# Decayed keys of 16 units turned by VectorE in 32 x 32 blocks and carried through DRAM

## The chip, the cores and the metric

The kernel runs on one core of one Trainium2 chip. Its time is the device time of one execution in microseconds (us), the median of several runs. TensorE (PE in the profile) multiplies, VectorE (DVE) and ScalarE (ACT) work on rows of up to 128 partitions, GpSimd (POOL) does a little of the same, and SyncE (SP) issues the DMAs in this kernel. Each engine works through its own instructions in their order and waits on semaphores for the others.

## What is computed

An attention with a state that decays channel by channel, and an MLP with ELU on its result. In the kernel the sequence is cut into chunks of 128 tokens, in which the decays are multiplied up, so that a chunk is a masked product of 128 x 128 scores, a product with the state, and an update of the state.

```python
def _attn_setup():
    batch, n_heads, seq, head_dim = (4, 8, 768, 48)
    ...

def _attn_ref(r, k, v, w, u) -> np.ndarray:
    B, H, S, D = r.shape
    state = np.zeros((B, H, D, D), dtype=np.float32)
    y = np.zeros_like(r)
    for t in range(S):
        kt, vt, rt, wt = (k[:, :, t], v[:, :, t], r[:, :, t], w[:, :, t])
        cur = np.einsum('bhd,bhe->bhde', u[None] * kt, vt)
        y[:, :, t] = np.einsum('bhd,bhde->bhe', rt, state + cur)
        state = wt[:, :, :, None] * state + np.einsum('bhd,bhe->bhde', kt, vt)
    return y.astype(np.float32)

def _moe_setup():
    n_tokens, d_model, d_ff = (3072, 384, 2048)
    ...

def _moe_ref(x, w_in, w_out) -> np.ndarray:
    h = x @ w_in
    alpha = 1.0
    g = np.where(h > 0.0, h, alpha * (np.exp(np.minimum(h, 0.0)) - 1.0))
    return (g @ w_out).astype(np.float32)

def reference(**kwargs):
    ...
    attn_out = _attn_ref(**attn_kwargs)
    B, H, S, D = attn_out.shape
    x = np.ascontiguousarray(attn_out.transpose(0, 2, 1, 3)).reshape(B * S, H * D)
    return _moe_ref(x=x, **moe_kwargs)
```

## The kernel before

A unit is one chunk c (6 of 128 tokens) of one batch b (4): unit i = 4c + b, 24 units. A unit holds 8 heads as 4 pairs p; a pair's two heads of 48 channels stand in 112 partitions (0 to 47 and 64 to 111; the rows between repeat channels of the first head). Keys and receptances come as `kr`, 112 channel rows of 4 x 128 tokens each, the decays as `w`, the values `v` in token rows.

Attention tasks of a unit, by the names that stand in the tables: `es` and `gs` (VectorE, scans that multiply up the decays, lines 435 and 445), `kh` and `rh` (VectorE, keys and receptances times them), `rk`, `rku`, `md`, `sp` (the diagonal with u), `s` (TensorE, scores, line 526), `mk` (VectorE, copy of the scores under the mask, two per unit, line 539), `t` (TensorE, four transposes that turn the decayed keys from channel rows to token rows in PSUM, line 544, for the units of chunks 0 to 4), `kt` (ScalarE, their copy to SBUF, line 549), `v` (TensorE, line 567, scores times values and state times receptances), `u` (TensorE, line 589, the outer products of keys and values, for two units at a time, named by the second), `up` (VectorE, state plus outer products), `pc` and `sc` (decay of the state), `xh` and `xl` (the result as a rounded part and a rest), `fl` (a check of the range).

The MLP runs over 105 steps n: `g1` (TensorE, line 263: 9 matmuls of one 128-wide slice f of the hidden layer), `r1`, `r2` (ScalarE), `stt` (VectorE, line 279), `gh` (ScalarE) and `gl` (VectorE, line 305), `g2` (TensorE, line 319: 9 matmuls into the sums `acc`). A chunk's 4 x 128 tokens are 512 columns; in chunks 0 and 1 the first slices are done in two halves of 256. The first five steps of chunk 0 use plain float32 (lines 269 and 294). The MLP of a chunk follows its attention, so that chunk c's MLP and chunk c + 1's attention share the engines.

The weights come as `raw` f (768 KB each, 16 of them) and are split into two parts: `a` (ScalarE), `cc` (VectorE, line 622), `wh` (ScalarE, line 627), `wl` (VectorE, line 631). These tasks lie in the first hundred microseconds; g1 of slice f needs wl f. raw 14 goes into a buffer that cc 11 frees, raw 15 into one that cc 12 frees.

Nothing is scheduled at run time. `ORDER` holds for each engine a line of task names, and each engine issues its tasks in that order; for SP the line holds the loads (`ld_w`, `ld_kr`, `ld_rk`, `ld_v`, `raw`) and the `store` of results. `Plan.order` merges the lines, and `hold` says which tasks must be done before a buffer is taken again (`SLOTS` counts the buffers: 3 of kr, 2 of kt, 5 PSUM banks `pa`). The last step of all is g2.104, behind which the last sums are copied and stored.

Of the kernel before, what the change touches and what calls it, by code (L numbers as in the profile page):

```python
# [8 lines left out]
F32 = mybir.dt.float32  # L9
# [10 lines left out]
B, H, S, D = 4, 8, 768, 48  # L20
DM, DFF = 384, 2048
P = 128
# [32 lines left out]
def _pieces():  # L55
    res = []
    for h in range(H):
# [15 lines left out]
UP = ["ACT"] * 4  # L73

# [6 lines left out]
SLOTS = dict(w=2, kr=3, rk=2, v=4, eg=2, md=2, am=2, kt=2, pa=5, wg=2, wt=2, m=2, gh=2, gl=2, x=2, acc=1, raw0=1, x0=1, x1=1, x1a=1, x1b=1, wl10=1, wl11=1, wl12=1, wl13=1, wl14=1, wl15=1)  # L81
# [8 lines left out]
    SP=(  # L90
# [261 lines left out]
def rwkv_elu_kernel(ctx, tc, wkr, rk, vp, u, gkrw, gv, gu, wp, out):  # L352
# [301 lines left out]
    for u_ in units:  # L654
# [35 lines left out]
        if c < NC - 1:  # L690
            add(("t", i), "PE", lambda u_=u_: trans(u_), [("kh", i), ("const",)])
            add(("kt", i), "ACT", lambda u_=u_: trans_out(u_), [("t", i)])
# [234 lines left out]
```

## Time and profile before

| | |
|---|---|
| runs of the kernel | 497.98, 498.17, 500.63 us; median 498.17 |
| the profiled execution | 499.62 us, its span 497.7 |
| TensorE clock granted | 0.998 of 2.4 GHz |
| TensorE busy | 489.3 us, 98 % |
| VectorE busy | 325.7 us, 65 % |
| ScalarE busy | 275.3 us, 55 % |
| GpSimd busy | 74.8 us, 15 % |

A busy share is an average over the span. The page's slices and the table by stretches tell how it is spread, and the list of waits tells for whom an engine stood still. Matmuls are pipelined: the records of neighbours overlap, and a pause shorter than the modelled end of a matmul is seen only in the starts. Where the text speaks of a step it means the time from one start to the next.

### The profile page before, as it was taken

The numbers are of one execution on the slowest core, as the hardware profiler recorded it, in microseconds if no ns is written. First come the engines' busy times: TensorE is split into PE (matmuls) and PEld (weight loads), VectorE is DVE, ScalarE is ACT, GpSimd is POOL, SyncE is SP. The second block draws the span as 40 slices with busy tenths as digits, with TensorE's granted clock in tenths as the row PEclk, the third lists the DMA queues.
The fourth block names the chain that finished last, engine by engine and source line by source line (L and its number), as shares of the span: only waits on it lengthen the run. The fifth ranks groups of instructions, "written<-read, shape, count | busy, mean of one in ns | idle before, by whom it ended". The sixth has DMA issues, their size and how long they took to land.

```text
span 497.7 us, 10425 instructions
## 1 busy us (share of the span) xinstructions
PE 489.3 (98%) x4305; PEld 412.3 (83%) x4305; DVE 325.7 (65%) x518; ACT 275.3 (55%) x553; POOL 74.8 (15%) x84
## 2 busy tenths in 40 slices
PE   8899999999999999999999999999999999999996
PEld 8689878789888888888888888888888888888885
DVE  6899999997888667647786478655562552324232
ACT  3999999776653444734453463444633444435434
POOL 3001032043004205113240341003000000000000
PEclk9999999999999999999999999999999999999999
DMA  8977864515223224225430423013112000010002
GB/s 277 299 262 244 291 227 148 159 52 146 62 73 95 65 69 148 78 61 169 118 101 22 126 96 112 0 39 109 43 24 79 1 3 0 20 46 1 0 0 68
DMA packets 18725, 48.96 MB, mean 98 GB/s; under 512 B 2160, under 2 KB 4336, under 8 KB 18672
## 3 DMA queue, kind: packets, MB, share of 16 engines
q1 hardware_dynamic: 18384, 47.84, 30.3%
q8 instruction: 36, 0.59, 0.5%
q10 hardware_dynamic: 288, 0.39, 0.2%
q14 instruction: 17, 0.14, 0.1%
HBM read 43.50 MB, written 4.72 MB: 97 GB/s over the span
## 4 chain that ended last, share of the span: by engine, by line


## 5 line engine op out<-in xcount | busy, mean ns | idle before, releaser
L263 PE MATMUL ph<-xh,w_h 128*128 128x512 f32 (+1 forms) x300 | 114.0, 380 | 0.0
L319 PE MATMUL acc<-gh,w_h 128*128 128x512 f32 (+1 forms) x299 | 113.4, 379 | 0.0
L319 PE MATMUL acc<-gl,w_h 128*128 128x512 f32 (+1 forms) x299 | 112.7, 377 | 0.1
L263 PE MATMUL ph<-xl,w_h 128*128 128x512 f32 (+1 forms) x300 | 112.7, 376 | 0.0
L263 PE MATMUL ph<-xh,w_l 128*128 128x512 f32 (+1 forms) x300 | 112.6, 375 | 0.0
L319 PE MATMUL acc<-gh,w_l 128*128 128x512 f32 (+1 forms) x299 | 112.3, 376 | 0.0
L279 DVE SCALAR_TENSOR_TENSOR m<-m,ph 128x512 f32<-128x512 f32 (+1 forms) x100 | 63.8, 647 | 72.9 <-ACT m L276 72.5
L305 DVE TENSOR_TENSOR gl<-m,gh 128x512 fp32r<-128x512 f32 (+1 forms) x100 | 65.8, 663 | 67.8 <-ACT gh L301 67.0
L301 ACT CAST gh<-m 128x512 fp32r<-128x512 f32 (+1 forms) x100 | 58.6, 590 | 90.9 <-PE acc L319 65.5
L273 ACT ACTIVATE m<-ph 128x512 f32<-128x512 f32 (+1 forms) x100 | 56.5, 568 | 88.6 <-PE ph L263 66.9
L319 PEld LDWEIGHTS acc<-gl,w_h 128*128 128x128 f32 x299 | 56.3, 188 | 10.9 <-DVE gl L305 0.9
L263 PEld LDWEIGHTS ph<-xh,w_h 128*128 128x128 f32 x300 | 56.5, 188 | 10.4 <-issue 0.2
L263 PEld LDWEIGHTS ph<-xh,w_l 128*128 128x128 f32 x300 | 56.5, 188 | 10.3
L319 PEld LDWEIGHTS acc<-gh,w_h 128*128 128x128 f32 x299 | 56.3, 188 | 10.4
L263 PEld LDWEIGHTS ph<-xl,w_h 128*128 128x128 f32 x300 | 56.5, 188 | 9.8
L319 PEld LDWEIGHTS acc<-gh,w_l 128*128 128x128 f32 x299 | 56.3, 188 | 10.1
L276 ACT ACTIVATE m<-m 128x512 f32<-128x512 f32 (+1 forms) x105 | 61.1, 594 | 1.4
L505 POOL TENSOR_SCALAR_AFFINE_SELECT am<-md 128x512 f32<-128x512 f32 x32 | 24.1, 776 | 156.2 <-PE pa_y L567 98.3
L464 POOL TENSOR_TENSOR rk<-rk 128x384 f32<-128x384 f32 x20 | 22.9, 1156 | 162.6 <-DMA rk<-in_rk_dram 115.7
L435 DVE TENSOR_TENSOR_SCAN eg<-w,reset 112x516 f32<-112x516 f32 x24 | 30.7, 1277 | 3.2 <-DMA w<-in_wkr_dram 1.8
L445 DVE TENSOR_TENSOR_SCAN eg<-w,reset 112x516 f32<-112x516 f32 x24 | 31.0, 1294 | 0.8
L539 DVE COPY_PREDICATED am<-upper,pa_s 128x512 f32<-128x512 uint32 x40 | 28.0, 730 | 5.2 <-PE pa_s L526 5.2
(86 smaller groups left out, 498.6 us busy)
## 6 DMA issues: line engine op xcount, KB each, us to landing
kr<-in_wkr_dram SPq DMA_DIRECT2D x23, 448.0 KB, 5.5
rk<-in_rk_dram SPq DMA_DIRECT2D x20, 384.0 KB, 3.4
wrawx<-in_wp_dram SPq DMA_DIRECT2D x10, 767.8 KB, 6.6
v<-in_vp_dram SPq DMA_DIRECT2D x24, 256.0 KB, 4.3
w<-in_wkr_dram SPq DMA_DIRECT2D x24, 226.2 KB, 3.8
wraw<-in_wp_dram SPq DMA_DIRECT2D x6, 767.8 KB, 4.5
out_dram<-o SPq DMA_DIRECT2D x9, 256.0 KB, 3.8
out_dram<-o SPq DMA_DIRECT2D x15, 128.0 KB, 2.2
```

Source lines behind the costliest of these rows:

```text
L263: nc.tensor.matmul(ph, w[f][:, 0, k], x_[:, k, :], start=(k == n == 0), stop=(k == NK - 1 and n == 2))
L273: act(s["m"], s["ph"], AF.Relu, scale=-1.0)
L276: act(s["m"], s["m"], AF.Exp, scale=-1.0)
L279: stt_(s["m"], s["m"], -1.0, s["ph"], ALU.add, ALU.max)
L301: nc.scalar.copy(s["gh"], s["m"])
L305: nc.vector.tensor_tensor(s["gl"], s["m"], s["gh"].bitcast(F32), ALU.subtract)
L319: nc.tensor.matmul(a_, w[f][:, 1, m], g[:, s_], start=(begin and n == 0), stop=(stop and n == 2))
L435: nc.vector.tensor_tensor_scan(out=flat(eg[:, 0]), data0=u_["w"][:, 1:W1][:, ::-1], data1=flat(reset[:, 0]), initial=0.0, op0=ALU.mult, op ...
L445: nc.vector.tensor_tensor_scan(out=flat(u_["eg"][:, 1]), data0=u_["w"][:, 0:W1 - 1], data1=flat(reset[:, 1]), initial=0.0, op0=ALU.mult, o ...
L464: eng.tensor_tensor(u_["rk"][:, 0], u_["rk"][:, 0], u_["rk"][:, 1], ALU.mult)
L505: nc.gpsimd.affine_select(out=am, in_=u_["md"][:, q::2].unsqueeze(2).broadcast_to([P, NP, C]), pattern=[[0, NP], [1, C]], compare_op=ALU.i ...
L539: nc.vector.copy_predicated(am.rearrange("t (z p) n -> t z p n", z=2), uppers, windows(pa))
```

## The change

For units 4 to 19 (`VIA`) the tasks `t` (TensorE) and `kt` (ScalarE) are replaced by three:

- `tr` (VectorE): one transpose instruction over 128 partitions and 512 columns, which turns each 32 x 32 block by itself. Its source is the decayed keys, read so that every fourth token makes a block; its target `kq` holds, for each block of 32 channels, token rows in 32 partitions. There is one buffer kq.
- `kd` (SP): a DMA that writes kq (256 KB) to a DRAM buffer.
- `kt` (SP): four DMAs, one for each block of 32 channels, that read it back with the 128 tokens in 128 partitions, in runs of 32 elements (128 bytes) in SBUF.

`kt` in SBUF is now 64 wide per head instead of 48. `kr` is loaded with 128 rows (16 rows repeated at the end) in these units, since the transpose works on whole blocks of 32. `u` waits for the new kt as it did for the old one. All lines of `ORDER` are new: besides the new names, the old ones stand in another order on every engine. The steps of the MLP are the same.

```diff
--- before.py
+++ after.py
@@ -71,6 +71,7 @@
 FILL = {('t', 0): 1, ('pd', 1): 5, ('s', 1): 3, ('g1', 0): 1}
 DIAG = ["PE"] * 4 + ["POOL"] * 20
 UP = ["ACT"] * 4
+VIA = [0] * 4 + [1] * 16 + [0] * 4
 
 
 F32A = 5
@@ -78,96 +79,97 @@
-SLOTS = dict(w=2, kr=3, rk=2, v=4, eg=2, md=2, am=2, kt=2, pa=5, wg=2, wt=2, m=2, gh=2, gl=2, x=2, acc=1, raw0=1, x0=1, x1=1, x1a=1, x1b=1, wl10=1, wl11=1, wl12=1, wl13=1, wl14=1, wl15=1)
+SLOTS = dict(w=2, kr=3, rk=2, v=4, eg=2, md=2, am=2, kt=2, kq=1, kd=4, pa=5, wg=2, wt=2, m=2, gh=2, gl=2, x=2, acc=1, raw0=1, x0=1, x1=1, x1a=1, x1b=1, wl10=1, wl11=1, wl12=1, wl13=1, wl14=1, wl15=1)
...
-        "raw.11 ld_kr.5 raw.12 ld_kr.7 ld_rk.6 raw.14 raw.13 ld_w.6 raw.15 ld_rk.7 ld_kr.6 ld_w.8 ld_v.7 ld_kr.10 ld_v.6 "
...
+        "raw.13 ld_w.6 ld_v.5 ld_kr.5 raw.12 ld_rk.6 kd.4 raw.14 kt.4 kd.5 raw.15 kt.5 ld_v.7 ld_v.6 ld_kr.6 ld_w.7 "
...
@@ -365,6 +367,7 @@
     ml = pool("ml", 3)
     ps_acc = pool("ps_acc", 1, space=PS)
     ps_h = ps_a = pool("ps_a", SLOTS["pa"], space=PS)
+    drm = pool("drm", 1, space=bass.MemoryType.DRAM)
     tt, stt, act = nc.vector.tensor_tensor, nc.vector.scalar_tensor_tensor, nc.scalar.activation
     flags = kp.tile([R2, NU], F32, name="flags")
     good = kp.tile([1, 1], I32, name="good")
@@ -415,16 +418,19 @@
         c, b = u_["c"], u_["b"]
         if n in WKR:
             lo, hi = WKR[n]
-            t, src = ld.tile([R2, hi - lo], F32, tag=n, name=n, bufs=SLOTS[n]), wkr[c, b, :, lo:hi]
+            rows = P if n == "kr" else R2
+            t, src = ld.tile([rows, hi - lo], F32, tag=n, name=n, bufs=SLOTS[n]), wkr[c, b, 0:rows, lo:hi]
         elif n == "rk":
             t, src = ld.tile([P, 2, DM], F32, tag=n, name=n, bufs=SLOTS[n]), rk[c, b]
         else:
             t, src = ld.tile([P, 4 * P], F32, tag=n, name=n, bufs=SLOTS[n]), vp[c, b]
         if n == "kr":
             m = K1 + R1 if u_["i"] else K1 + R1 + 2 * NP
-            nc.sync.dma_start(t[:, 0:m], src[:, 0:m])
-            u_["k"], u_["r"] = (t[:, x:x + K1].rearrange("d (p t) -> d p t", p=NP) for x in (0, K1))
-            u_["ru"] = t[:, K1 + R1:]
+            rows = P if VIA[u_["i"]] else R2
+            nc.sync.dma_start(t[0:rows, 0:m], src[0:rows, 0:m])
+            u_["kx"] = t[:, 0:K1]
+            u_["k"], u_["r"] = (t[0:R2, x:x + K1].rearrange("d (p t) -> d p t", p=NP) for x in (0, K1))
+            u_["ru"] = t[0:R2, K1 + R1:]
         else:
             nc.sync.dma_start(t, src)
             u_[n] = t
@@ -544,9 +550,24 @@
             nc.tensor.transpose(pt[:, p], u_["k"][:, p, :], ident[0:R2, 0:R2])
 
     def trans_out(u_):
-        u_["kt"] = at.tile([P, NP, 2, D], F32, tag="kt", name="kt", bufs=SLOTS["kt"])
+        u_["kt"] = at.tile([P, NP, 2, 64], F32, tag="kt", name="kt", bufs=SLOTS["kt"])[:, :, :, 0:D]
         x = u_["pt"][:, :, 0:2 * D].rearrange("t p (z d) -> t p z d", z=2)
         nc.scalar.copy(u_["kt"], bass.AP(x.tensor, x.offset, [*x.ap[0:2], [64, 2], x.ap[3]]))
+
+    def blocks(u_):
+        u_["kq"] = t = at.tile([P, 4, NP, 32], F32, tag="kq", name="kq", bufs=SLOTS["kq"])
+        nc.vector.transpose(t.rearrange("t z p d -> t p z d"), u_["kx"].rearrange("d (p t z) -> d p z t", p=NP, z=4))
+
+    def blocks_out(u_):
+        u_["kd"] = t = drm.tile([P, 4, NP, 32], F32, tag="kd", name="kd", bufs=SLOTS["kd"])
+        nc.sync.dma_start(t, u_["kq"])
+
+    def blocks_in(u_):
+        t = at.tile([P, NP, 2, 64], F32, tag="kt", name="kt", bufs=SLOTS["kt"])
+        for z in range(4):
+            nc.sync.dma_start(t[:, :, z // 2, z % 2 * 32:z % 2 * 32 + 32],
+                              u_["kd"][32 * z:32 * z + 32].rearrange("t z p d -> (t z) p d"))
+        u_["kt"] = t[:, :, :, 0:D]
 
     def scale_state(u_):
         tt(st[:, u_["b"]], st[:, u_["b"]], u_["pc"].broadcast_to([R2, NP, 2 * D]), ALU.mult)
@@ -688,8 +709,13 @@
         for q in range(2):
             add(("mk", i, q), "DVE", lambda u_=u_, q=q: mask(u_, q), [("s", i), ("sp", i)])
         if c < NC - 1:
-            add(("t", i), "PE", lambda u_=u_: trans(u_), [("kh", i), ("const",)])
-            add(("kt", i), "ACT", lambda u_=u_: trans_out(u_), [("t", i)])
+            if VIA[i]:
+                add(("tr", i), "DVE", lambda u_=u_: blocks(u_), [("kh", i)])
+                add(("kd", i), "SP", lambda u_=u_: blocks_out(u_), [("tr", i)])
+                add(("kt", i), "SP", lambda u_=u_: blocks_in(u_), [("kd", i)])
+            else:
+                add(("t", i), "PE", lambda u_=u_: trans(u_), [("kh", i), ("const",)])
+                add(("kt", i), "ACT", lambda u_=u_: trans_out(u_), [("t", i)])
         after = [("mk", i, 0), ("mk", i, 1), ("ld_v", i)]
         if c > 0:
             add(("sc", i), "DVE", lambda u_=u_: scale_state(u_), [("pc", i), ("up", ALONG[i - B])])
@@ -753,7 +779,7 @@
         hold("x%d" % (c % 2), ("v", B * c), g1s)
     for u_ in units:
         i, c = u_["i"], u_["c"]
-        for n, users in dict(w=["es", "gs"], kr=["s", "t", "kh", "rh"] + ["v"] * (c > 0), rk=["md"], v=["v", "u"]).items():
+        for n, users in dict(w=["es", "gs"], kr=["s", "t", "tr", "kh", "rh"] + ["v"] * (c > 0), rk=["md"], v=["v", "u"]).items():
             hold(n, ("ld_" + n, i), [(x, ALONG[i] if x == "u" else i) for x in users] + [("ubd",)] * (n == "kr" and i == 0))
         hold("eg", ("es", i), [("fl", i), ("rh", i), ("kh", i)] + [("pc", i)] * (c > 0))
         hold("md", ("md", i), [("sp", i)] + [("zst",)] * (i == 0))
@@ -764,7 +790,9 @@
         hold("pa", ("s", i), [("mk", i, 0), ("mk", i, 1)], 2)
         hold("pa", ("v", i), [("xh", i), ("xl", i)] + [("xf", i)] * (i < (4 if F32B else 2 if F32A else 0)))
         hold("pa", ("t", i), [("kt", i)])
-        hold("kt", ("t", i), [("u", ALONG[i])])
+        hold("kt", ("kt" if VIA[i] else "t", i), [("u", ALONG[i])])
+        hold("kq", ("tr", i), [("kd", i)])
+        hold("kd", ("kd", i), [("kt", i)])
         hold("pa", ("u", i), [("up", i)])
     for f in range(NF):
         p = "raw0" if f % 3 == 0 or f == NF - 1 else "x1a" if f % 3 == 1 else "x1b"
@@ -902,6 +930,7 @@
         uz[z, 0:D, :, z] = inputs["u"].reshape(NP, 2, D)[:, z].T
     uz = np.broadcast_to(uz.reshape(P, 2 * NP)[0:R2], (NC, B, R2, 2 * NP))
     wkr = np.concatenate([x.reshape(NC, B, R2, -1) for x in (w, k, r, uz)], axis=-1)
+    wkr = np.concatenate([wkr, wkr[:, :, 0:P - R2]], axis=2)
     n_it = S // GT
     gen = lambda x: x.reshape(B, NP, 2, n_it, GT, D).transpose(3, 2, 4, 0, 1, 5).reshape(n_it, 2, -1)
     gkrw = np.concatenate([gen(inputs[n]) for n in "krw"], axis=2)
```

On TensorE, the end of the scores of unit 6 and what follows them (L526 and L532 are the scores, L544 the transposes, L263 and L265 g1.21); before:

```order
L526 MATMUL pa_s<-kr 64x128 x2
L526 MATMUL pa_s<-kr 64x64 x2
L544 MATMUL pa_t<-ident,kr 128x112 x4
L263 MATMUL ph<-xh,w_h 128x256
L263 MATMUL ph<-xl,w_h 128x256
L263 MATMUL ph<-xh,w_l 128x256
```

and now:

```order
L532 MATMUL pa_s<-kr 64x128 x2
L532 MATMUL pa_s<-kr 64x64 x2
L265 MATMUL ph<-xh,w_h 128x256
L265 MATMUL ph<-xl,w_h 128x256
L265 MATMUL ph<-xh,w_l 128x256
```

The four transposes are gone, and the step of the MLP follows the scores.

On VectorE, from the scan of unit 5's decays to the mask of unit 4 (L445 and L451 are the scans, L622 and L643 `cc`, L631 and L652 `wl`, L559 the transpose tr.5); before:

```order
L445 SCALAR_TENSOR_TENSOR eg<-w,reset 112x516
L449 TENSOR_TENSOR kr<-kr,eg 112x512
L279 SCALAR_TENSOR_TENSOR m<-m,ph 128x512 x2
L305 TENSOR_TENSOR gl<-m,gh 128x512
L631 SCALAR_TENSOR_TENSOR w_l<-wg,w_h 128x768
L471 TENSOR_REDUCE md<-rk 128x8
L622 SCALAR_TENSOR_TENSOR wg<-wraw,wt_100 128x768
L305 TENSOR_TENSOR gl<-m,gh 128x512
L539 COPY_PREDICATED am<-upper,pa_s 128x512
```

and now:

```order
L451 SCALAR_TENSOR_TENSOR eg<-w,reset 112x516
L281 SCALAR_TENSOR_TENSOR m<-m,ph 128x512
L559 STREAM_TRANSPOSE kq<-kr 128x4x4x32
L643 SCALAR_TENSOR_TENSOR wg<-wraw,wt_101 128x768
L652 SCALAR_TENSOR_TENSOR w_l<-wg,w_h 128x768
L281 SCALAR_TENSOR_TENSOR m<-m,ph 128x512
L307 TENSOR_TENSOR gl<-m,gh 128x512
L545 COPY_PREDICATED am<-upper,pa_s 128x512
L573 TENSOR_TENSOR st<-st,pc 112x384
```

tr.5 stands in front of cc.12; the multiply of the receptances (L449, rh.5) has moved behind the mask, and md.5 further ahead.

On SP, the last loads of weights (wraw and wrawx are `raw`); before:

```order
L425 DMA kr<-in_wkr_dram 112x1024
L429 DMA rk<-in_rk_dram 128x768
L609 DMA wrawx<-in_wp_dram 128x3071 x2
L429 DMA w<-in_wkr_dram 112x517
L609 DMA wraw<-in_wp_dram 128x3071
L429 DMA rk<-in_rk_dram 128x768
L425 DMA kr<-in_wkr_dram 112x1024
```

and now:

```order
L435 DMA rk<-in_rk_dram 128x768
L563 DMA kd<-kq 128x512
L630 DMA wrawx<-in_wp_dram 128x3071
L568 DMA kt<-kd 128x4x32 x4
L563 DMA kd<-kq 128x512
L630 DMA wraw<-in_wp_dram 128x3071
L568 DMA kt<-kd 128x4x32 x4
L435 DMA v<-in_vp_dram 128x512 x2
L430 DMA kr<-in_wkr_dram 128x1024
```

The writes and reads of units 4 and 5 stand between raw.14, raw.15 and the loads of units 6 and 7.

## Rows read from the trace of the kernel before

**Rows 1.** The page, parts 1 and 2: busy shares, and VectorE in 40 slices.

```profile
PE 489.3 (98%) x4305; PEld 412.3 (83%) x4305; DVE 325.7 (65%) x518; ACT 275.3 (55%) x553; POOL 74.8 (15%) x84
...
DVE  6899999997888667647786478655562552324232
```

**Rows 2.** Waits of TensorE: line, whom it waited for, us in total, times, longest.

```profile
PE pa_y L567 <- DVE am L536: 1.6, 1, 1.6
...
PE ph L269 <- ACT xf L578: 0.2, 1, 0.2
```

**Rows 3.** Stretches: length, then busy us of PE, PEld, DVE, ACT, POOL, clock, DMA.

```profile
40.00:88.00 48.00, 47.88 (x465) 40.92 (x463) 46.01 (x68) 44.92 (x89) 7.19 (x6) 1.00 0.66 223
88.00:125.00 37.00, 36.91 (x368) 32.45 (x367) 32.46 (x56) 26.70 (x65) 10.27 (x10) 1.00 0.38 111
...
200.00:350.00 150.00, 150.00 (x1374) 125.09 (x1373) 97.17 (x152) 68.88 (x130) 32.44 (x34) 1.00 0.28 85
```

**Rows 4.** TensorE in order of time, v.4, v.5 and g2.15: start, us, line, operation.

```profile
81.68 1.06 PE L567 MATMUL pa_y<-am,v 128*32 128x128 f32 x32
...
83.21 1.58 PE L567 MATMUL pa_y<-am,v 128*32 128x128 f32 x32
...
87.75 0.39 PE L319 MATMUL acc<-gh,w_h 128*128 128x512 f32 x1
88.21 0.50 PE L319 MATMUL acc<-gl,w_h 128*128 128x512 f32 x1
```

**Rows 5.** VectorE in order of time from gl.15 to rh.6.

```profile
87.48 0.68 DVE L305 TENSOR_TENSOR gl<-m,gh 128x512 fp32r<-128x512 f32 x1
...
89.34 0.68 DVE L305 TENSOR_TENSOR gl<-m,gh 128x512 fp32r<-128x512 f32 x1
89.94 0.95 DVE L622 SCALAR_TENSOR_TENSOR wg<-wrawx,wt 128x768 uint32<-128x768 uint32 x1
90.81 0.68 DVE L449 TENSOR_TENSOR kr<-kr,eg 112x512 f32<-112x512 f32 x1
```

**Rows 6.** TensorE in order of time, the transposes of unit 6 and g1.21.

```profile
103.36 0.60 PE L544 MATMUL pa_t<-ident,kr 112*128 112x112 f32 x4
103.73 0.36 PE L263 MATMUL ph<-xh,w_h 128*128 128x256 f32 x1
```

**Rows 7.** Groups by line and form: count, busy us, mean ns; idle before: the copies of the transposes.

```profile
L549 ACT COPY kt<-pa_t 128x384 f32<-128x384 f32 x20 | 9.5, 474 | 7.9 <-PE pa_t L544 7.9
```

**Rows 8.** TensorE in order of time, from MLP matmuls to scores and back.

```profile
393.47 0.39 PE L263 MATMUL ph<-xl,w_h 128*128 128x512 f32 x1
393.69 0.39 PE L263 MATMUL ph<-xh,w_l 128*128 128x512 f32 x1
394.01 0.90 PE L526 MATMUL pa_s<-kr 48*64 48x128 f32 x32
394.84 0.50 PE L319 MATMUL acc<-gh,w_h 128*128 128x512 f32 x1
395.18 0.40 PE L319 MATMUL acc<-gl,w_h 128*128 128x512 f32 x1
```

**Rows 9.** Groups by line and form on VectorE: a scan and two kinds of multiply.

```profile
L445 DVE TENSOR_TENSOR_SCAN eg<-w,reset 112x516 f32<-112x516 f32 x24 | 31.0, 1294 | 0.8
...
L449 DVE TENSOR_TENSOR kr<-kr,eg 112x512 f32<-112x512 f32 x24 | 17.6, 737 | 0.0
...
L456 DVE TENSOR_TENSOR kr<-kr,eg 112x256 f32<-112x256 f32 x20 | 10.0, 502 | 1.4 <-DMA kr<-in_wkr_dram 1.2
```

**Rows 10.** The page, part 6: DMA issues, count, KB each, median us to landing.

```profile
v<-in_vp_dram SPq DMA_DIRECT2D x24, 256.0 KB, 4.3
...
out_dram<-o SPq DMA_DIRECT2D x9, 256.0 KB, 3.8
out_dram<-o SPq DMA_DIRECT2D x15, 128.0 KB, 2.2
```

**Rows 11.** DMA queue of SP from 493.2 to 497.7 us: packets, MB, share of 16 engines.

```profile
q1 hardware_dynamic: 288, 0.39, 24.9%
```

161 rows, old and new, of tables (ACT, DVE, PE, POOL) are left out of this document.

## The prediction

> **What bounds the kernel now.** I read the page's busy shares first: TensorE is busy for 489.3 of 497.7 us at the full clock, VectorE for 65 per cent, and the slices show where they meet: VectorE is at 9 tenths in nearly all of the first ten and at 5 to 7 from then on [rows 1]. Then the waits of TensorE: beside its warm-up the profile names 1.6 us of v.1 for the mask and 0.2 us of g1.0 for xf, both in the start [rows 2]. So after the start the end is set by the sum of what TensorE has to do. The table by stretches splits this in two. From 200 to 350 us TensorE is busy without a break and VectorE has a third of its time free; but from 40 to 88 us VectorE is busy for 46.01 of 48 us and ScalarE for 44.92 [rows 3]. In that stretch, where the weights are split into their parts, all three engines are full, and TensorE already pays for it. A TensorE gap that is shorter than a matmul's modelled end is not shown as idle, so I read starts: the second half of v.5 runs 1.58 us where the same 32 matmuls of v.4 took 1.06, and the first matmul of g2.15 is followed after 0.46 us [rows 4], not after the 0.22 of an unhindered one [rows 8]. Those two are 0.5 + 0.2 = 0.7 us of waiting, and the second is for gl.15, which VectorE ends at 88.16 us [rows 5]. Hence a microsecond of TensorE is worth a microsecond late in the span, and before it only as far as VectorE lets it.
>
> **What goes from TensorE.** Sixteen units lose their four transposes. Their price is the step to the next start, not the mean duration: the group of unit 6 starts at 103.36 and the next matmul at 103.73, 0.37 us [rows 6]. 16 x 0.37 = 5.9 us. A second term comes from the order. Between two MLP matmuls a step is 0.22 to 0.23 us. Into a group of scores it is 0.32, and the first MLP matmul after such a group takes 0.34: some 0.20 us for every change of kind and back [rows 8]. In TensorE's table the attention work from u.3 on stands in 20 places between MLP work before, and in 16 now. 4 x 0.20 = 0.8 us. Both terms lie on the path that sets the end.
>
> **What comes to VectorE.** Sixteen transposes of 128 x 512. The trace has none. From below, 512 columns as two instructions of 256 (line 456) take 2 x 0.50 us, and from above a scan of 516 columns takes 1.29 us; one pass over 512 columns with one result per column takes 0.74 (line 449) [rows 9] or 0.68 (line 305) [rows 5]. I take 0.7 us, of which some 0.62 occupy the queue, since neighbours overlap: behind an instruction of 0.68 us the next one starts after 0.60, behind one of 0.95 after 0.87 [rows 5]. The eleven that stand behind gl.26 are some 7 us in the rest of the span, and they lie in the free third.
> The Trainium skill (VectorE: DVE Perf Modes, "The three transpose paths") gives 390 ns for a 128 x 128 bf16 transpose on TensorE and 311 ns on VectorE. TensorE's rows here show 0.37 us for four, so that figure is not a price in a stream. Four times 311 ns would be an estimate of 1.24 us for a unit, and with the two that stand ahead of gl.15 the sum would come out 1.2 us later, at 493.5.
>
> **The full stretch, 40 to 125 us.** Ahead of gl.15 VectorE now has tr.4 and tr.5 (1.24 us) and, by exchanges of neighbours in its table, cc.14 and wl.13 for cc.15 and stt.16 (0.95 + 0.95 against 0.95 + 0.68, 0.3 us): 1.5 us more. TensorE has two groups of transposes and one change of kind fewer ahead of g2.15 (0.9 us), so it arrives earlier and the work that it waits for ends later. If VectorE keeps its 2 us of idle time in 40 to 88 us [rows 3], the wait at g2.15 grows by 1.5 + 0.9 = 2.4 us; if the transposes fill that idle time (ScalarE, full as well, loses two copies of 0.47 us there [rows 7]) it grows by 0.6. I take **1.5 us**. Three more (tr.6, tr.7, tr.9) stand ahead of gl.26. In 88 to 125 us VectorE is busy for 32.46 of 37 us [rows 3], so 1.9 us fit there, and I add nothing; the bound is one more wait of 1.5 us.
>
> **The start.** pd.2 and u.1 now stand ahead of g1.0. Before, they followed it. Put into the waits of v.1 and g1.0 they save at most those 1.6 + 0.2 = 1.8 us [rows 2]. But ScalarE now does fl.0 ahead of md.0 and VectorE's first loads come in another order, so part of it goes into other waits (I find stt.0 and rkc.3 late by half a microsecond or more). I take **0.7 us**, with 0 and 1.8 as ends.
>
> **SP and the road through DRAM.** Each unit adds a write of 256 KB and four reads of 64 KB, 80 issues of some 0.4 us in a queue that is mostly idle, and its kr load grows from 448 to 512 KB. kd.4 waits on SP for tr.4, and raw.14 is queued behind it; but raw.14 itself needs the buffer that cc.11 frees, and cc.11 stands behind tr.4 on VectorE. The same holds for kd.5, raw.15 and cc.12. Both cost nothing. Behind kt.5, which waits until kd.5 has landed, stand the loads of unit 6 and 7, and kr.6 needs a buffer that v.4 frees later anyway. The arrival at TensorE is what counts. From tr.5's end VectorE has 8.0 us of work to the masks of unit 5 (three instructions of 768 columns at 0.87, seven of 384 to 512 at 0.60 [rows 5], a scan at 1.2), then v.5 takes 1.6, so u.5 wants kt.5 some **9.6 us** after tr.5. The chain is a write (256 KB stored: 3.8 us [rows 10]), four issues (1.7) and the landing. For that 256 KB loaded in rows of 2 KB take 4.3 us from issue [rows 10]; from above, the small packets of the kernel's last stores take 24.9 per cent of 16 x 4.5 us for 288, 62 ns each [rows 11], and 2048 pieces of 128 bytes over 16 engines at that price are 8.0 us on top of the 2.2 us of a small store [rows 10]. So 9.8 to 15.7 us, and u.5 would wait 0.2 to 6 us. Up to 2.4 us of that is hidden, since TensorE would stand at g2.15 a task later. I take the lower end, as the same bytes lie nearest, and price the wait at nothing. The other seven pairs have 16 us and more between their last transpose and their u.
>
> **Sum.** 498.2 - 5.9 - 0.8 + 1.5 - 0.7 = **492.3 us** for the median of the runs. The profiled execution took 499.6 (span 497.7 and 1.9 around it), 1.4 above the median, and by the same sum its like would be 493.7.
>
> **Rivals.**
> - **Nothing new waits.** The transposes fill VectorE's idle time and the start gives its 0.7: 490.8. For it: 2 us idle in the stretch and ScalarE eased. Against it: g2.15 waits already [rows 4].
> - **u.5 waits for its keys.** At 62 ns a piece u.5 is late by 6 us, 2.4 of them hidden: 492.3 + 3.6 = 495.9. For it: 2048 pieces of 128 bytes behind a weight load of 768 KB (raw.15) in one queue. Against it: the 1.37 KB packets of the row move ten times a piece's bytes. The Trainium skill (DMA: Bandwidth & Descriptors, "Specifications") asks for at least 512 bytes for full rate, which speaks for this rival; no row here has a piece of 128 bytes in bulk.
> - **The transpose is slow, and the kernel slower than before.** It reads columns four words apart and writes blocks; at two scans' price (2.56 us) five of them in the full stretch add 5 x 1.94 = 9.7 us: 502.0. The gain is eaten from 5.9 / 5 + 0.62 = 1.8 us a transpose on. Against it: every one-pass instruction in the trace runs at one column a step.
> - **The order alone.** Loads on SP stand behind kd and kt, and VectorE's waits grow by some 4 us in all: 496 to 498, no change that can be told.
>
> **How the numbers follow.** Forecast 0.53, nothing new waits 0.22, u.5 late 0.13, slow transpose 0.06, order 0.06. The range goes from 490.0 (the start gives more) to 496.8 (g2.15 at 2.4, no gain at the start, a second wait of 1.5, two transposes at a scan's price, 1.2). A measurement here tells some 0.5 per cent (2.5 us) from no change: faster means below 495.7, which holds for the first two cases and about a third of the late u.5: 0.80; same 0.13; slower 0.07.
>
> **What would show it.** TensorE's records 64 fewer, its busy time about 6 us less; a transpose on VectorE of 0.65 to 0.8 us; the wait at g2.15 of 1 to 3 us and at u.5 of none; from 125 us on no wait on TensorE. The prediction is wrong if a transpose takes over 1.3 us, if u waits for kt anywhere, or if VectorE waits for a load that stands behind kd or kt on SP.

## The result and the profile after

The changed kernel takes 492.92 us (median of 7 runs, 492.62 to 495.41) against 498.17 for the kernel before; the ratio is 0.9898, 95 % interval 0.9871 to 0.9924. That is 5.25 us less, where 5.9 were forecast (492.3 us). The profiled execution took 492.90 us with a span of 491.3. In some executions of the new kernel, and of kernels with its start, TensorE's clock falls to half in the start (between 14 and 28 us in the three traces that caught it) and the run takes 3 to 8 us longer; medians below contain some of these, so single steps are compared in the traces, behind that stretch.

The page of the changed kernel, busy us and VectorE in 40 slices (before: [rows 1]):

```profile
PE 483.2 (98%) x4241; PEld 406.2 (83%) x4241; DVE 345.6 (70%) x534; ACT 267.2 (54%) x537; POOL 77.5 (16%) x84
...
DVE  6999999998788877578776857965574535133432
```

TensorE has 64 records and 6.1 us less, VectorE 19.9 us more. The stretches, columns as in [rows 3]:

```profile
40.00:88.00 48.00, 47.77 (x456) 40.48 (x455) 47.60 (x71) 42.71 (x86) 0.63 (x2) 1.00 0.73 236
88.00:125.00 37.00, 35.59 (x364) 31.34 (x363) 33.93 (x58) 25.87 (x64) 9.96 (x10) 1.00 0.49 137
200.00:350.00 150.00, 150.00 (x1388) 124.84 (x1388) 109.29 (x162) 67.79 (x130) 33.73 (x34) 1.00 0.38 107
```

From 40 to 88 us VectorE is now busy for 47.60 of 48 us: the transposes did fill the 2 us that it had left. TensorE loses 1.41 us between 88 and 125, where it lost 0.09 before. The waits of TensorE (before: [rows 2]):

```profile
PE acc L408 <- POOL ident masks.py:199: 1.7, 1, 1.7
PE pa_y L588 <- issue: 1.0, 1, 1.0
PE ph L265 <- DVE st L619: 0.4, 1, 0.4
PE acc L296 <- DVE m L291: 0.2, 1, 0.2
PE pa_d L487 <- DVE rkc L482: 0.2, 1, 0.2
PE ph L265 <- DVE w_l L652: 0.2, 1, 0.2
```

The first is the warm-up. The 1.6 us of v.1 for the mask are gone. New are 0.2 for w_l (wl.11 ahead of g1.16), 0.4 behind an update of the state (up.5 ahead of g1.19) and 1.0 us of "issue", a wait that no semaphore explains. None is where I had put it: at g2.15 TensorE runs through. TensorE in order of time, the end of v.5, u.5, g1.17 and g2.15:

```profile
81.15 1.06 PE L588 MATMUL pa_y<-am,v 128*32 128x128 f32 x32
82.14 0.92 PE L610 MATMUL pa_u<-v,kt 128*48 128x48 f32 x32
83.00 0.50 PE L265 MATMUL ph<-xh,w_h 128*128 128x512 f32 x1
...
85.17 0.39 PE L321 MATMUL acc<-gh,w_h 128*128 128x512 f32 x1
85.39 0.40 PE L321 MATMUL acc<-gl,w_h 128*128 128x512 f32 x1
```

Beside [rows 4]: the second half of v.5 is back at 1.06 us and the first step of g2.15 at 0.22. And u.5 starts the moment v.5 is done, so the road through DRAM is hidden.

A second series of the changed kernel stood beside e6 to e8 as a yardstick:

> The changed kernel itself once more, as the yardstick for the three that follow: 492.5 to 493.5.

It gave 493.49 us (0.9911, 0.9878 to 0.9945). To tell the start from the rest I use one figure for every kernel: the time from the start of g1.5 (the first matmul of the sixth MLP step) to the start of the last g2. It is worked out from the starts in each trace; the changed kernel, profiled twice, gave 446.33 and 446.59, so a difference under 0.3 us says nothing.

| kernel | g1.5 starts at | g1.5 to last g2 | v.7 | v.10 + v.11 | median of runs |
|---|---|---|---|---|---|
| before | 40.21 | 450.89 | 1.65 | 3.20 | 498.17 |
| changed | 38.35 | 446.33 | 3.07 | 3.84 | 492.92 |
| changed, again | 46.12 | 446.59 | 2.85 | 3.99 | 493.49 |
| e1 order alone | 39.55 | 458.78 | 1.64 | 3.20 | 507.12 |
| e2 ballast | 38.94 | 450.98 | 1.65 | 3.20 | 498.19 |
| e3 double, ahead of 125 us | 39.03 | 449.70 | 2.86 | 3.94 | 497.60 |
| e4 double, behind 125 us | 38.67 | 452.21 | 2.30 | 6.84 | 499.33 |
| e6 masks first | 38.65 | 446.80 | 3.35 | 3.21 | 493.20 |
| e7 swaps | 38.93 | 447.02 | 3.10 | 4.01 | 493.96 |
| e8 code moved | 46.58 | 445.30 | 1.64 | 3.89 | 495.10 |
| e9 three edits | 42.63 | 444.46 | 1.64 | 3.21 | 497.44 |
| e10 order before | 39.47 | 460.56 | 1.65 | 3.74 | 508.73 |
| e11 keys late | 38.61 | 454.08 | 1.72 | 4.19 | 501.81 |
| e12 three edits, start kept | 39.37 | 445.13 | 1.64 | 3.21 | 493.85 |

So behind the start the change is worth 450.89 - 446.33 = 4.56 us; the forecast for that part was 5.9 + 0.8 - 1.5 = 5.2.

### The profile page after: what moved, and what is told of

Its sections match the earlier page's. It is cut to its first block, busy times and chain, and to the rows that moved or that the text cites. A ratio compares the mean times of both kernels' runs of the same rounds, so it can differ in the third digit from the quotient of the medians.

```text
span 491.3 us, 10417 instructions
## 1 busy us (share of the span) xinstructions
PE 483.2 (98%) x4241; PEld 406.2 (83%) x4241; DVE 345.6 (70%) x534; ACT 267.2 (54%) x537; POOL 77.5 (16%) x84
## 4 chain that ended last, share of the span: by engine, by line
## 5 line engine op out<-in xcount | busy, mean ns | idle before, releaser
L265 PE MATMUL ph<-xh,w_h 128*128 128x512 f32 (+1 forms) x300 | 114.1, 380 | 0.4 <-DVE st L619 0.4
L265 PE MATMUL ph<-xh,w_l 128*128 128x512 f32 (+1 forms) x300 | 113.0, 377 | 0.2 <-DVE w_l L652 0.2
L265 PE MATMUL ph<-xl,w_h 128*128 128x512 f32 (+1 forms) x300 | 112.7, 376 | 0.0
L307 DVE TENSOR_TENSOR gl<-m,gh 128x512 fp32r<-128x512 f32 (+1 forms) x100 | 70.6, 715 | 45.1 <-ACT gh L303 44.6
L265 PEld LDWEIGHTS ph<-xh,w_l 128*128 128x128 f32 x300 | 56.4, 188 | 11.6 <-DVE w_l L652 1.3
L265 PEld LDWEIGHTS ph<-xh,w_h 128*128 128x128 f32 x300 | 56.5, 188 | 11.5 <-PE acc L321 0.8
L265 PEld LDWEIGHTS ph<-xl,w_h 128*128 128x128 f32 x300 | 56.5, 188 | 9.8
L470 POOL TENSOR_TENSOR rk<-rk 128x384 f32<-128x384 f32 x20 | 24.6, 1234 | 185.6 <-DMA rk<-in_rk_dram 185.6
L451 DVE TENSOR_TENSOR_SCAN eg<-w,reset 112x516 f32<-112x516 f32 x24 | 31.1, 1295 | 0.8
```

The source lines that it names most:

```text
L265: nc.tensor.matmul(ph, w[f][:, 0, k], x_[:, k, :], start=(k == n == 0), stop=(k == NK - 1 and n == 2))
L307: nc.vector.tensor_tensor(s["gl"], s["m"], s["gh"].bitcast(F32), ALU.subtract)
L451: nc.vector.tensor_tensor_scan(out=flat(u_["eg"][:, 1]), data0=u_["w"][:, 0:W1 - 1], data1=flat(reset[:, 1]), initial=0.0, op0=ALU.mult, o ...
L470: eng.tensor_tensor(u_["rk"][:, 0], u_["rk"][:, 0], u_["rk"][:, 1], ALU.mult)
```

## Experiments

### TensorE's work given back

The four transposes of each of the sixteen units run again on TensorE, into the tile of the scores, which overwrite them.

```
+        for p in range(NP * VIA[u_["i"]]):
+            nc.tensor.transpose(pa[0][:, p, 0:R2], u_["k"][:, p, :], ident[0:R2, 0:R2])
```

> The changed kernel with TensorE's work put back as ballast: for each of units 4 to 19 the four transposes run ahead of the scores into the scores' own PSUM tile and are overwritten; VectorE's transposes, the road through DRAM and all tables stay. Theory A (the sum of TensorE's work): +6.0 to 6.5 us, 498.9 to 499.4. Theory B (TensorE's time was covered): 493 to 494.5.

498.19 us, 0.9999 of the kernel before (0.998 to 1.0018); 450.98 us behind g1.5, again that of the kernel before. The page, and TensorE in order of time at unit 6:

```profile
PE 489.3 (99%) x4305; PEld 413.0 (83%) x4305; DVE 346.0 (70%) x534; ACT 267.5 (54%) x537; POOL 77.7 (16%) x84
```

```profile
101.01 0.55 PE L519 MATMUL pa_s<-ident,kr 112*128 112x112 f32 x4
101.49 0.90 PE L534 MATMUL pa_s<-kr 48*64 48x128 f32 x32
```

Theory A holds: TensorE's time was not covered by waits, and with its 64 records back the gain is gone. The median lies 0.7 us under A's range. By the starts in the traces, the sixteen groups take 0.48 to 0.53 us each, 8.0 in all, but only 4.65 arrive behind g1.5: v.7, v.10 and v.11 give 2.06 back and the MLP steps 1.26. TensorE now comes later to VectorE's results; at v.7 it is its code that has moved (see below). That the sum meets the kernel before to 0.1 us is in part chance: the groups cost 1.5 us more than the transposes that they stand for (6.47), and the steps of the MLP and of v take 1.7 less than before. So the new order, the relieved ScalarE, the road through DRAM and VectorE's 17.5 us of transposes are together worth some 1.5 us in e2, and the greater part of the gain is TensorE's work.

### The transposes doubled

The instruction is issued twice, for units 4, 5, 6, 7 and 9 (e3) or for the other eleven (e4).

```
+        for _ in range(2 if u_["i"] in (4, 5, 6, 7, 9) else 1):
             nc.vector.transpose(...)
```

> The changed kernel with VectorE's transpose done twice for units 4, 5, 6, 7 and 9, those that stand ahead of 125 us: 5 x 1.0 us more of VectorE where it is full, and keys 1 us later. Theory A (VectorE is charged in the full stretch, less what idle time it has left there, 0.4 us of 48 in 40 to 88 and 3.1 of 37 in 88 to 125): 494.4 to 496.4. Rival, VectorE has room even there: 492.4 to 493.4. Rival, all of it is charged: 497.9.

> The changed kernel with VectorE's transpose done twice for the other eleven units (8, 10 to 19), all behind 125 us: 11 x 1.0 us more of VectorE where it has a third of its time free. Theory A: nothing, 492.4 to 493.5. Rival, VectorE's queue is in the chain there as well: up to 503.9, and anything above 495 speaks for it.

e3 takes 497.60 us, e4 499.33: both cost, and the one that was to be free costs more. In the traces, behind g1.5, it is 3.4 us for five (0.67 each) and 5.9 for eleven (0.53 each). The largest of TensorE's waits in each, first e3's, then e4's:

```profile
PE ph L265 <- DVE w_l L653: 2.5, 2, 1.3
```

```profile
PE pa_y L589 <- DVE am L545: 2.9, 3, 2.2
```

e3 lies above theory A's 494.4 to 496.4 and just under the 497.9 of the rival by which all of it is charged; by the traces it is two thirds. A weight part (wl) comes later there by what stands ahead of it, and VectorE's idle time hid less than A had thought. e4 refutes A for the "free third". VectorE is idle there for a third of the time, but tr.11 stands directly ahead of the masks of unit 11. VectorE in e4 at that place, and e4's stretches behind it:

```profile
174.67 2.26 DVE L560 STREAM_TRANSPOSE kq<-kr 128x512 f32<-128x512 f32 x2 [2.35 <-DMA kd<-kq]
176.84 0.70 DVE L545 COPY_PREDICATED am<-upper,pa_s 128x512 f32<-128x512 uint32 x1
```

```profile
174.00:177.50 3.50, 1.43 (x53) 1.16 (x44) 2.80 (x4) 0.48 (x1) 2.00 (x3) 1.00 0.75 232
177.50:181.50 4.00, 3.91 (x82) 3.37 (x86) 3.66 (x6) 0.48 (x1) 2.15 (x3) 0.58 1.00 279
```

TensorE stood for 2.2 us, and then its granted clock was 0.58 for four microseconds (mostly the 1.2 GHz level), some 1.7 us more: this wait was paid for almost twice, and the 5.9 us hold that too.

### One transpose moved behind the masks

The changed kernel shows the same place in small. VectorE, then TensorE, in order of time:

```profile
173.65 1.14 DVE L559 STREAM_TRANSPOSE kq<-kr 128x512 f32<-128x512 f32 x1 [2.39 <-DMA kd<-kq]
174.71 0.70 DVE L545 COPY_PREDICATED am<-upper,pa_s 128x512 f32<-128x512 uint32 x1
```

```profile
175.47 0.86 PE L588 MATMUL pa_y<-kr,st 112*32 112x128 f32 x24
176.15 1.47 PE L588 MATMUL pa_y<-am,v 128*32 128x128 f32 x32
```

tr.11 waits 2.39 us for the one kq buffer, which kd.10 has to empty first, with the masks behind it, and the second half of v.11 takes 1.47 us.

```
+ORDER["DVE"] = ORDER["DVE"].replace(" tr.11 mk.11.0 xl.8 mk.11.1 ", " mk.11.0 xl.8 mk.11.1 tr.11 ")
```

> The changed kernel with one step of VectorE's table moved: tr.11 behind the two masks of unit 11 instead of ahead of them. In the changed kernel tr.11 stands 2.39 us for its one buffer (kd.10 has to land first) and v.10, v.11 and s.12 together take some 0.7 us longer than their like. Theory A (a transpose is charged where it stands ahead of a mask that TensorE wants): v.11 takes 1.6 us instead of 2.08, the end 0.5 to 0.7 us earlier. Rival, the stretch there is a load of TensorE's code (one landed at 178): no change, v.11 stays above 2.0 us.

TensorE in e6, the two halves of v.11:

```profile
176.67 0.84 PE L590 MATMUL pa_y<-kr,st 112*32 112x128 f32 x24
177.33 1.06 PE L590 MATMUL pa_y<-am,v 128*32 128x128 f32 x32
```

v.11 takes 1.65 us instead of 2.08 and v.10 1.56 instead of 1.76, so at this place theory A holds and 0.63 us come back. At the end they don't show: v.7 took 0.28 longer in this execution, some steps moved by 0.2 to 0.4, and the median (493.20) can't be told from the changed kernel's.

### The waits of the full stretch

```
+ORDER["DVE"] = ORDER["DVE"].replace(" wl.15 up.5 ", " up.5 wl.15 ").replace(" tr.5 cc.12 wl.11 ", " wl.11 tr.5 cc.12 ")
```

> The changed kernel with two steps of VectorE's table moved in the full stretch: wl.11 ahead of tr.5 and cc.12, and up.5 ahead of wl.15. Theory A (there TensorE waits for VectorE's next instruction and for nothing else): the 0.33 us ahead of the second matmul of g1.16 and the 0.54 us ahead of g1.19 go, the end is 0.6 to 0.9 us earlier. Rival, the wait moves to the next step that VectorE serves (g2.15, g1.20): no change.

Both waits go (g2.14 and g1.19 start 0.54 us earlier each, against the steps ahead of them), but u.5 and g1.18 start 0.37 and 0.43 later: in front of the masks of unit 5 VectorE now waits 0.47 us for ScalarE, and the wait for gl.15 at g2.15 is back (its first step takes 0.53 us). That is the rival: in this stretch, where all three engines are full, the wait removed turns up at the next step. The median of 493.96 is no gain. Why the wait at g1.19 was there at all is seen in VectorE and GpSimd of the changed kernel side by side:

```profile
87.67 1.30 DVE L307 TENSOR_TENSOR gl<-m,gh 128x512 fp32r<-128x512 f32 x1 [0.16 <-ACT gh L303]
88.90 1.77 DVE L652 SCALAR_TENSOR_TENSOR w_l<-wg,w_h 128x768 fp32r<-128x768 f32 x1
```

```profile
87.41 2.44 POOL L470 TENSOR_TENSOR rk<-rk 128x384 f32<-128x384 f32 x2 [47.37 <-DMA rk<-in_rk_dram]
89.81 2.72 POOL L473 TENSOR_TENSOR rk<-rk,ub 128x384 f32<-128x384 f32 x2
```

While GpSimd multiplies rows, an instruction of 0.69 us takes 1.30 and one of 0.95 takes 1.77. The load for rk.7 now stands behind kt.5 on SP and arrives in the middle of the full stretch, and rk.6 stands behind rk.7 on GpSimd; before, GpSimd did this work at 68 and 81 us. No run took this overlap away; that it makes up.5 late is read from the rows alone.
The Trainium skill (SBUF — State Buffer, "Who interferes with whom") says that a VectorE instruction with two SBUF inputs and a GpSimd instruction that reads SBUF lock each other out of a shared port; these rows agree, with 1.43 us for the two.

### A wait without a semaphore

In the changed kernel the last four matmuls of v.7 come late, and the trace names nobody. TensorE in order of time, and the instruction queue (q8, 16 KB a packet, TensorE's code) in two windows, 89.5 to 110.3 and 110.3 to 115 us:

```profile
110.55 1.04 PE L588 MATMUL pa_y<-am,v 128*32 128x128 f32 x28
112.62 0.41 PE L588 MATMUL pa_y<-am,v 128*32 128x128 f32 x4 [1.03 <-issue]
```

```profile
q14 instruction: 1, 0.01, 0.2%
```

```profile
q8 instruction: 2, 0.03, 2.6%
```

From 87.8 to 110.4 us, 227 matmuls, no block of code was loaded; on average one comes per 125 or so. The next follows 3.3 us later. s.7, v.6 and v.7 stand side by side in TensorE's table and run 144 matmuls in 4 us. (Two other blocks come after 221 and 211 matmuls and nothing is seen to wait for them; why this one was late was not settled.) To test it, all later code is moved by a few matmuls:

```
+            for _ in range(16 if k == ("pd", 1) else 0):
+                nc.tensor.matmul(first["accs"]()[0][0:32, 0:2], ident[:, 0:32], ident[:, 0:2], start=True, stop=True)
```

> The changed kernel with sixteen matmuls of two columns added in a wait of the start (ahead of pd.1), which moves every later block of TensorE's code by sixteen matmuls. In the changed kernel the last four matmuls of v.7 start 1.3 us late; they wait for no semaphore, and a 16 KB instruction load was seen at 110.4 us, 227 matmuls after the one before it where some 125 are usual. Theory A (TensorE ran out of code): that wait goes or turns up elsewhere, v.7 takes 1.6 us instead of 3.07, and the end is 0.8 to 1.3 us earlier, less at most 0.4 for the added matmuls. Rival, v.7 waits for data (a mask, v or the state): v.7 still takes 3.0 us, no change.

TensorE in e8, the second half of v.7 and the step behind it:

```profile
118.60 1.06 PE L588 MATMUL pa_y<-am,v 128*32 128x128 f32 x32
119.59 0.39 PE L265 MATMUL ph<-xh,w_h 128*128 128x256 f32 x1
```

v.7 takes 1.64 us. It takes 2.85 to 3.35 in the changed kernel, its second profile, e3, e6 and e7, which have the same code up to there (2.30 in e4; 1.72 in e11, where TensorE stood still at u.5 first), and 1.64 in e9 and e12 below, which move the code by sixteen records of matmuls instead of e8's 32; e1 and e2, whose transposes of units 4 to 7 move it by sixteen records too, have 1.64 and 1.65. In these five the block is loaded 107 to 127 matmuls after the one before it. Where the code is not moved, the wait without a semaphore grows with the block's lateness: none after 180 matmuls (e11), 0.26 us after 200 (e4), 0.81 after 211 (e3), 1.03 after 227 and 1.30 after 235 (e6); and TensorE goes on 2.2 to 2.5 us after the block's load begins. So it was code, not data, and it costs the changed kernel 1.2 to 1.4 us. The time of a whole run shows no gain: the profiled execution had the half clock in the start (g1.5 at 46.58), three of the six runs had a mean clock of 0.986 to 0.993, and the median is 495.10.

### The road through DRAM made longer

The reads of unit 5's keys are issued four times over.

> The changed kernel with the keys of unit 5 read from DRAM four times over, one behind the other: twelve more issues of some 0.65 us, so kt.5 lands 7.8 us later or more, and the loads behind it too. It prices the slack of the road: in the changed kernel kt.5's last read is issued at 76.5 us and a read takes 3.3 us to land, so u.5 at 82.1 has 2.3 us in hand. Theory A: u.5 waits for the rest, 5.5 us or more, and the end comes 3.5 to 6 us later, 496.5 to 499. Rival (u.5 can wait without harm, or the slack is larger): 492.5 to 494.

501.81 us (two runs; 1.0071, 1.0044 to 1.0098), more than either theory said, and the wait that the forecast's second rival meant, followed by the stretch from 89 to 94 us:

```profile
PE pa_u L610 <- DMA kt<-kd: 6.4, 2, 5.6
```

```profile
89.00:94.00 5.00, 4.17 (x23) 3.40 (x23) 1.76 (x3) 0.00 (x0) 0.00 (x0) 0.50 0.85 259
```

The mechanism is real: u.5 waits as soon as the reads are late, and the end is later by 7.8 us behind g1.5. Theory A's 3.5 to 6 left out that TensorE runs at the 1.2 GHz level behind such a wait, as in e4: an MLP step takes 0.43 us there instead of 0.23. In the changed kernel the wait is not reached. SP at tr.5 and the medians from issue to landing between 64 and 82 us:

```profile
72.52 0.33 SPq L563 DMA_DIRECT2D kd<-kq  x1
73.36 0.33 SPq L630 DMA_DIRECT2D wraw<-in_wp_dram  x1
74.58 2.55 SPq L568 DMA_DIRECT2D kt<-kd  x4
```

```profile
kd<-kq SPq DMA_DIRECT2D x2, 256.0 KB, 2.8
kt<-kd SPq DMA_DIRECT2D x8, 64.0 KB, 3.3
```

From tr.5's end (72.50) the last read is issued at 76.5 and should land near 79.8 (an estimate from these medians), some 7.3 us, and u.5 starts at 82.14.

### Each half alone

In e1 the transposes go back to TensorE and ScalarE under the new tables; in e10 the sixteen units go through VectorE and DRAM under the old ones.

```
-VIA = [0] * 4 + [1] * 16 + [0] * 4
+VIA = [0] * 24
+for i in range(4, 20):
+    x = {8: 'u.7', 10: 'u.9', 12: 'u.11', 13: 'u.11', 16: 'u.15', 18: 'u.17'}.get(i, f"s.{i}")
+    ORDER["PE"] = ORDER["PE"].replace(f" {x} ", f" {x} t.{i} ")
+    ...
```

> The order alone: the changed kernel's tables, with the transposes of units 4 to 19 back on TensorE (behind the unit's scores, or behind the u that frees its key buffer) and the copies on ScalarE; no transpose on VectorE, no road through DRAM. Theory A, the end is set by the sum of TensorE's work: sixteen groups of four transposes come back at 0.37 to 0.40 us, 6.0 to 6.5 us, and some 1.5 us of new waits of the changed kernel may go: 497 to 499. The new start stays, so the second-half step g1.5 begins near 38.4 us as in the changed kernel and not at 40.2. Theory B, the gain came from the new order and the transposes were covered by waits: 493 to 494.5.

> The change without its new tables: the order of the kernel before, with only what the change needs edited in it (the sixteen transposes taken from TensorE's table and the copies from ScalarE's, each tr right behind its kh on VectorE, each kd and kt on SP near the time at which its transpose was done). Theory A (the sum of TensorE's work, and a transpose charged where VectorE is full): 498.5 - 6.2 + 16 transposes at 0.25 to 0.6 us = 496 to 502, so most of the gain needs the new tables. Rival (VectorE takes them wherever they stand): 492 to 493.

507.12 and 508.73 us: either half alone is slower than both kernels, and beyond every range that was given for it. The largest waits of TensorE in e1, then in e10:

```profile
PE pa_t L558 <- DVE st L627: 2.1, 2, 1.3
PE pa_t L558 <- DVE m L289: 1.9, 1, 1.9
```

```profile
PE acc L327 <- DVE gl L313: 6.6, 11, 1.5
```

In e1 the transposes wait for a PSUM tile: they take one of the five "pa" tiles that scores, values and MLP steps share, and the new order has none to spare at those places. That place I chose by a rule, so e1 is no price of the order and its question stays open. In e10 a transpose stands right behind its kh, and eleven times a gl that TensorE wants comes late by it. VectorE's time in e10 is free for a third as well. What makes it usable is the table.

### Three edits together

e9 joins tr.11 behind its masks, up.5 ahead of wl.15 and the moved code; e12 does the same but leaves the start alone and puts its eight small matmuls ahead of g2.0.

```
+ORDER["DVE"] = ORDER["DVE"].replace(" wl.15 up.5 ", " up.5 wl.15 ")
+ORDER["DVE"] = ORDER["DVE"].replace(" tr.11 mk.11.0 xl.8 mk.11.1 ", " mk.11.0 xl.8 mk.11.1 tr.11 ")
+            for _ in range(8 if k == ("g2", 0) else 0):
+                nc.tensor.matmul(first["accs"]()[0][0:32, 0:2], ident[:, 0:32], ident[:, 0:2], start=True, stop=True)
```

> The changed kernel with three edits at once: tr.11 behind the masks of unit 11 (0.6 us came back there when done alone), up.5 ahead of wl.15 (0.5 us ahead of g1.19), and TensorE's code moved on by sixteen matmuls (three of the start's five filling matmuls kept, ten of two columns put in the place of the other two), since 32 more took 1.5 us out of v.7. Theory A (the waits left behind 40 us are these three and each is worth its length): 2.0 to 2.6 us less than the changed kernel, 490.3 to 491.2 where the start runs like the changed kernel's. Rival (each wait moves to the next late step): 492.3 to 493.5.

> The three edits of the run before (tr.11 behind the masks of unit 11, up.5 ahead of wl.15, TensorE's code moved on by sixteen instructions of its own), but with the start left as the changed kernel has it: the added eight matmuls of two columns stand ahead of g2.0, where TensorE waits half a microsecond, and not in the place of filling matmuls ahead of pd.1. Theory A (the three waits are worth their length, and the run before lost it to a TensorE clock that fell to half in the start): 490.6 to 491.6. Rival, the clock falls with any such edit, or the waits come back: 493 or more.

Behind g1.5 e9 takes 444.46 us and e12 445.13, which is 1.2 to 1.9 less than the changed kernel, where 2.0 to 2.6 were expected; v.7, v.10 and v.11 are at their shortest in both. As whole kernels they gain nothing that can be told: e9 497.44, e12 493.85 (0.9907, 0.9875 to 0.9938). In e9 that is the clock in the start; in e12 the mean clock of three runs speaks for it, but no trace of one was kept. In e9 two of five filling matmuls ahead of pd.1 had given way to matmuls of two columns, and the stretches read:

```profile
12.00:14.00 2.00, 2.00 (x24) 1.78 (x24) 2.00 (x3) 1.97 (x9) 0.35 (x1) 0.90 1.06 372
14.00:20.00 6.00, 6.00 (x58) 5.01 (x58) 4.39 (x8) 4.00 (x11) 0.00 (x0) 0.50 0.81 292
```

All twelve runs of e9 had a mean clock of 0.981 to 0.993. Of the changed kernel's fifteen runs three had less than 0.99, and the others 0.997 to 1.0. Three of e12's six runs had 0.991 to 0.993 and took 494.97 to 495.72 us; the others took 491.73 to 492.74. A version that surely beats the changed kernel was not found.

## Why the prediction was right, point by point

The time came out; of the five signs that the forecast named two came (64 records and 6.1 us less on TensorE, no wait at u.5) and three did not (the price of a transpose, the wait at g2.15, no wait behind 125 us). The range's upper end adds up to 496.6, not 496.8.

**What goes from TensorE.** Forecast 5.9 us, and this is what the change is worth. The groups of transposes in TensorE's starts sum to 8.21 us for twenty before and 1.74 for the four that stay, 6.5 less; as the scores' groups now take their entry from the MLP themselves (0.3 more in sum), some 6.2 net, 0.39 a unit where the step of [rows 6] gave 0.37. e2 shows that giving it back takes the gain away.

**The changes of kind.** Forecast 0.8. All MLP steps together take 402.35 us before and 402.76 after, by the starts. With the waits among them taken out (0.24 us at g2.15 before; 0.33, 0.54 and 0.2 at g1.16, g1.19 and g2.0 after) 402.1 and 401.7 are left. So the term has the sign and half the size; no run measured it alone. The count behind it was off by one: TensorE's table before has 21 such places from u.3 on, not 20, so that its own price would have given 1.0.

**The price on VectorE.** This was the worst-sized term: 0.7 us taken, 1.10 measured. The group by line, and tr.4 with its neighbour:

```profile
L559 DVE STREAM_TRANSPOSE kq<-kr 128x512 f32<-128x512 f32 x16 | 17.5, 1096 | 3.8 <-DMA kd<-kq 3.8
```

```profile
63.66 1.08 DVE L559 STREAM_TRANSPOSE kq<-kr 128x512 f32<-128x512 f32 x1
64.66 0.92 DVE L652 SCALAR_TENSOR_TENSOR w_l<-wg,w_h 128x768 fp32r<-128x768 f32 x1
```

It occupies the queue for 1.00 us, not 0.62. I went by an instruction that reads and writes in rows ([rows 9]); this one reads columns four words apart and is nearer to two instructions of 256 columns (2 x 0.50) or to the scan (1.29), the bounds that I had named. Whether the stride or the transposing sets its price, no run shows.
The Trainium skill (VectorE: DVE Perf Modes, "The three transpose paths") led to an estimate of 1.24 us a unit from its 311 ns; measured are 1.10, nearer than my 0.7.

**The full stretch.** Forecast 1.5 us lost; 2.2 were lost, but not there and not by that. g2.15 does not wait. VectorE's idle time was filled, which is the case behind the lower bound (0.6 there; 2.4 less the 2 us of idle time would be 0.4). What is left of VectorE's lateness are the two waits at g1.16 and g1.19, together 0.9 us, against the 0.7 us at v.5 and g2.15 that went: 0.2 net. The rest is v.7's 1.4 us, which are code, and 0.6 at v.10 and v.11, which come from the single kq buffer. I had followed kd on SP as a wait of SP (raw.14 behind it), and not the wait that it makes for the next tr: VectorE stood 3.8 us for it, in two places. That two causes that were not in the sum stand in for one that did not come is luck.

**The free third.** "Nothing" for eleven transposes is too low by those 0.6 us, and as a rule it is wrong: in e4 a second one there costs 0.5 us on the mean, most of it where it stands ahead of a mask that TensorE wants next, and in e10 it is the gl behind the transposes that TensorE waits for. Free time in a stretch is a mean; what counts is which instruction stands behind.

**The start.** Forecast 0.7. In the traces g1.5 starts at 38.35 us instead of 40.21, 1.9 less, but the profiled execution of before was 1.4 us over its median; and g1.5 of kernels with the new start lies anywhere from 38.3 to 39.6 where the clock held. From the medians, 5.25 - 4.56 = 0.7 would be left for it. The 1.6 us of v.1 for its mask are gone, as expected.

**SP and the road.** Right, with an easy chain: 7.3 us where I had 9.8 to 15.7, since the small reads land in 3.3 us, sooner than the 4.3 of a load in rows that I had taken. The 62 ns a piece of [rows 11], from a few packets at the kernel's end, was no price for bulk. One sign of being wrong did come by the letter, a load behind kd on SP for which VectorE waits:

```profile
DVE kr L455 <- DMA kr<-in_wkr_dram: 4.6, 1, 4.6
```

That is rh.21 at 342 us; es.19 waits 1.4 us for its w at 247 us in the same way. But the writes ahead of the two loads (kd.18, kd.15) had been issued 16 and 15 us before them, and what held SP between was a buffer that TensorE frees (13.8 us for v, 14.9 us for u):

```profile
SPq L430 <- PE pa_y L588: 13.8, 1, 13.8
```

TensorE waited at neither place.

**The rivals.** "Nothing new waits" (490.8) would have been nearly right for VectorE's part of the full stretch; the code block and kq kept it away. "u.5 waits" has its mechanism (e11), some 2.3 us of slack away. "Slow transpose": the price came out at 1.10, between my value and the threshold of 1.8. e3 and e4 double it, to over 2 us of queue, and cost 3.4 and 5.9 us behind g1.5; both at once would by their sum end behind the kernel before, but that was not run. "The order alone" is not what e1 measured.

## What to carry to other kernels

When one engine is full to the end, price a step taken from it by start-to-start times, and expect just that; then ask of every step that another engine takes on not how busy that engine is, but which instruction stands next behind the new one and who waits for it. Count a single buffer as a wait for its writer too, with the transfer that empties it. A gap in which the full engine waits for no semaphore may be its own code: look at the instruction queue, and move the code by a few instructions before looking for a cause in the data.

## What the runs showed of the hardware

- TensorE can stand without a semaphore because its code comes late: in a burst of short matmuls (144 in some 4 us) a block that came at 110.4 us, 227 matmuls after the last, cost 1.2 to 1.4 us, and moving the code by sixteen records of matmuls took it away.
- A VectorE instruction with two inputs stretched from 0.69 to 1.30 us and from 0.95 to 1.77 while GpSimd multiplied rows.
- TensorE's granted clock fell to the 1.2 GHz level after a wait of 2.2 us in the middle of the kernel (0.58 over the next 4 us in e4), during the waits at u.5 in e11 (0.50 from 89 to 94 us), and for 7 to 14 us in the start of some executions. With two of five filling matmuls there replaced by ones of two columns all of twelve runs had a lowered mean clock. What exactly sets it off in the others was not found.
- Reads of 64 KB from DRAM in pieces of 128 bytes landed 3.2 us after their issue (median of 64; 3.3 between 64 and 82 us).
